# Three expert layers on one Trainium2 core: side work and low parts issued behind a row's first eviction, cosine chains shifted by a few turns

## The chip, the cores and the metric

The kernel runs on one core of one Trainium2 chip. The metric is the device time of one execution in microseconds (us), the median of several runs. The engines are TensorE (PE; its weight loads are listed as PEld), VectorE (DVE), ScalarE (ACT), GpSimd (POOL) and SyncE (SP), whose queue issues the DMAs.

## The reference, cut to what matters

```
attn = windowed attention with a linear bias, 4 batches, 8 heads, 576 positions   -> x [2304, 512]
P    = exp(x @ w_gate - max), then 8 rounds of row and column normalisation       -> P [2304, 8]
out  = sum over 8 experts e of  P[:, e:e+1] * (relu(x @ w1[e]) @ w2[e])            # w1 [512,1024], w2 [1024,512]
h    = out @ w_in                                                                   # [512, 2048]
y    = (h * cos(h)) @ w_out                                                         # [2048, 512]
```

`w_in` and `w_out` arrive as 64-bit floats.

## The kernel before, in words

After the attention stage come 120 steps in a fixed order: three token blocks of 768 tokens through the experts (32 units of 256 hidden columns each, 96 steps), then the same three blocks through the cosine layer (8 units each, 24 steps). All operands are split into a high part (rounded by a ScalarE copy) and a low part (the rest, a subtraction on VectorE or GpSimd), and every product is three matmuls: high by high, high by low, low by high.

**One step.** The first layer of a unit is a Strassen-like scheme of seven products (`product`, called with m = 5, 1, 4, 2, 3, 6, 7) of six matmuls of 384 columns each, recorded on line 759. Product 4 belongs to the unit of the step before. Between product 6 and product 7 stands `batch`: the second layer (`g2`) of an earlier unit, one step back for the experts and two for the cosine layer. It has six rows of 128 tokens (tt = 0 to 5), each of six matmuls of 512 columns (lines 863 to 865) into one PSUM bank of the pool `p_g`, which has three banks, and then one eviction (`evac`): line 854 (experts) or 844 (cosine layer) adds it to the accumulator on VectorE. Row 3 therefore needs the bank of row 0 to be read, row 4 that of row 1, and so on. All other orders are written by hand: each engine executes its instructions in the order in which the program issues them.

**After product 6** the first half of the hidden values is complete (an addition on VectorE, line 792). For the experts `relu_split` makes its high part on ScalarE (line 720) and its low part on VectorE (line 721), in front of row 0. In the cosine layer a chain (`cos_chain`) is put on the list `tail`; each call of `tick` advances every chain by one turn (up to the next `yield`): a scaled copy on ScalarE (line 731), a pair on VectorE (733, 736), the sine on ScalarE (739), a product on VectorE (742), the high part on ScalarE (746), the low part on GpSimd (748). The second half has its own chain, put there at product 4.

**Side work** stands in lists of generators, and `slot()` advances the first one of each list by one call: `pre` (splitting the weights of coming units while block 0 runs: `prep_s` on GpSimd, `prep_a` with line 132 on VectorE, `prep_b` with line 145 on GpSimd), `feed` (what the next token block needs), `bg` (first the eight normalisation rounds, whose matmul is `cs` on line 348; then `convert_f64`, which makes 32-bit weights from the 64-bit ones with seven VectorE operations, lines 218 to 238, one chunk a step) and `bg2` (splitting these weights). A slot follows each of the seven products and each of the six rows; the rows advance `pre` once more. What is left in `pre` at the end of a step is flushed. In the last step of a token block `combos` splits the next block's operands (lines 293 and 294) behind products 1, 2, 3, 6 and 7. At the end of the program two batches are left.

Of the kernel before, what the change touches and what calls it, by code (L numbers as in the profile page):

```python
# [29 lines left out]
def tile_attention_moe_cos_ffn(ctx, tc, q, k, v, w_gate, w1, w2, w_in, w_out, out):  # L30
    nc = tc.nc
    B, H, S, D = q.shape
    NT, DM = out.shape
    E, _, F = w1.shape
# [5 lines left out]
    NU1 = E * UPE  # L40
    NU2 = DFF // FU
# [8 lines left out]
    TB = 2 * HB  # L50
    NB = NT // TB
# [19 lines left out]
    with tc.manual_schedule():  # L71
# [508 lines left out]
        for hp in range(NPAIR):  # L580
            for j in range(2):
                h = 2 * hp + j
# [28 lines left out]
        for n in range(NGR + 6):  # L611
            if n < NGR:
                pi, u = groups[n]
# [76 lines left out]
        bg, bg2, pre, feed = [], [], [], []  # L690

        def step_all(lst):
            if lst and next(lst[0], StopIteration) is StopIteration:
                lst.pop(0)

        def lazy(f):
            yield from f()

        def slot():
            step_all(pre)  # L700
            step_all(feed)
            step_all(bg)
            step_all(bg2)
# [12 lines left out]
                    nc.scalar.activation(out=t[:, kc, h * HB:(h + 1) * HB], in_=ps[:, :HB], func=AF.Copy)  # L716
                    yield

        def relu_split(c, h, cols):
            nc.scalar.activation(out=h[:, 0, cols], in_=c, func=AF.Relu)  # L720
            nc.vector.scalar_tensor_tensor(  # L721
                out=h[:, 1, cols], in0=c, scalar=0.0, in1=h[:, 0, cols].bitcast(F32),
                op0=ALU.max, op1=ALU.subtract,
            )

        def cos_chain(c, new_h, tag):
            yield
            yield
            ta = u_pool.tile([P, TB], F32, tag=tag, name="ta")
            tb = u_pool.tile([P, TB], F32, tag="u0", name="tb")  # L730
            nc.scalar.activation(out=ta, in_=c, func=AF.Identity, scale=1.0 / TWO_PI, bias=quarter)
            yield
            nc.vector.tensor_scalar(
                out=tb, in0=ta, scalar1=MAGIC, scalar2=MAGIC, op0=ALU.add, op1=ALU.subtract
            )
            nc.vector.tensor_tensor(out=ta, in0=ta, in1=tb, op=ALU.subtract)
            yield
            yield
            nc.scalar.activation(out=ta, in_=ta, func=AF.Sin, scale=TWO_PI_LO)
            yield  # L740
            yield
            nc.vector.tensor_tensor(out=c, in0=c, in1=ta, op=ALU.mult)
            yield
            yield
            h = new_h()
            nc.scalar.activation(out=h[:, 0], in_=c, func=AF.Copy)  # L746
            yield
            nc.gpsimd.tensor_tensor(out=h[:, 1], in0=c, in1=h[:, 0].bitcast(F32), op=ALU.subtract)  # L748
# [16 lines left out]
        h_t = {}  # L765
# [3 lines left out]
        def product(s, m):  # L769
            kind, b, u = s  # L770
            nm = f"{kind}{b}_{u}"
            if s not in st_t:
                st_t[s] = {}
            t = st_t[s]
            lo, hi = slice(0, HB), slice(HB, TB)

            def bank(key):
                if key not in t:
                    t[key] = (p_y if key == "y" else p_xz).tile([P, 512], F32, tag=key, name=f"{key}_{nm}")
                return t[key]  # L780

            def cc(f):
                if f not in t:
                    t[f] = tp2.tile([P, TB], F32, tag=f"c{f}", name=f"c{f}_{nm}")
                return t[f]

            def keep(i, ps):
                t["s", i] = tp1.tile([P, HB], F32, tag=f"s{i}", name=f"s{i}_{nm}")
                nc.scalar.activation(out=t["s", i], in_=ps[:, :HB], func=AF.Copy)  # L789

            def add(o, ps, i):
                nc.vector.tensor_tensor(out=o, in0=ps[:, :HB], in1=t["s", i], op=ALU.add)  # L792

            def h(f):
                if (s, f) not in h_t:
                    h_t[s, f] = hp_.tile([P, 2, TB], F32R, tag=f"h{f}", name=f"h{f}_{nm}")
                return h_t[s, f]

            ps = bank({2: "x", 5: "z", 3: "z"}.get(m, "y"))
            unit_mm(ps, s, m, m in (1, 2, 5), m in (4, 2, 3))  # L800
            if m == 5:
                keep(3, ps)
            elif m == 1:
                keep(1, ps)
            elif m == 2:
                add(cc(1)[:, lo], ps, 1)
            elif m == 6:
                keep(2, ps)
                if kind == "moe":
                    add(cc(1)[:, hi], t["z"], 2)  # L810
                    relu_split(cc(1), h(0), slice(0, TB))
                else:
                    add(cc(1)[:, hi], t["z"], 2)
                    tail.append(cos_chain(cc(1), lambda: h(0), "u1"))
            elif m == 7:
                add(cc(2)[:, hi], ps, 3)
                if kind == "moe":
                    relu_split(cc(2)[:, hi], h(1), hi)
            elif m == 4:
                if kind == "moe":  # L820
                    relu_split(ps[:, :HB], h(1), lo)
                else:
                    nc.scalar.activation(out=cc(2)[:, lo], in_=ps[:, :HB], func=AF.Copy)
                    tail.append(cos_chain(cc(2), lambda: h(1), "u2"))
                del st_t[s]

        tail = []
# [40 lines left out]
        steps = []  # L868
# [18 lines left out]
        def begin_b(n):  # L887
            if n >= len(steps):
                return
            kind, b, u = steps[n]  # L890
            if b or kind == "ffn":
                load_w(u, b, "b")
            else:
                pre_next.append(prep_b(u))

        def tick():
            tail[:] = [t for t in tail if next(t, StopIteration) is not StopIteration]
# [4 lines left out]
        queue = []  # L902
        rest = []

        def batch():
            m = queue.pop(0)
            for tt in range(TPB):
                g2(steps[m], tt)
                if tt == TPB - 1:
                    begin_b(m + 2)  # L910
                slot()
                step_all(pre)
                tick()

        for n, s in enumerate(steps):
            kind, b, u = s
            pre += pre_next
            pre_next.clear()
            ph = phases.index((kind, b))
            last = n + 1 == len(steps) or steps[n + 1][:2] != (kind, b)  # L920
            nxt = phases[ph + 1] if ph + 1 < len(phases) else None
            to_end = (NU1 if kind == "moe" else NU1 + NU2) - u
            if nxt and to_end == 4:
                if nxt[0] == "ffn":
                    feed.append(x2_pieces(nxt[1]))
                    feed.append(lazy(lambda nxt=nxt: stages(nxt, x2r[nxt[1]])))
                else:
                    feed.append(stages(nxt, xr[nxt[1]]))
            nx = None
            if last and nxt:  # L930
                while feed:
                    step_all(feed)
                nx = combos(nxt, xr[nxt[1]] if nxt[0] == "moe" else x2r[nxt[1]])
            lag = 1 if kind == "moe" else 2
            for m in (5, 1, 4, 2, 3, 6, 0, 7):
                if m == 0:
                    if queue and queue[0] <= n - lag:
                        batch()
                    continue
                if m == 4:  # L940
                    if n:
                        product(steps[n - 1], 4)
                    for x in rest:
                        next(x, None)
                    rest.clear()
                    begin(n + 1)
                else:
                    product(s, m)
                tick()
                slot()  # L950
                if nx and m not in (5, 4):
                    next(nx, None)
            if nx:
                next(nx, None)
                rest.append(nx)
            queue.append(n)
            if chunk < 4 * NU2 and ((kind, b) == ("moe", 1) and u < NU1 - 5 or (kind, b) == ("moe", 2)):
                bg.append(convert_f64(chunk))
                chunk += 1
            at = n - NU1  # L960
            if 0 < at <= 5 * NU2 and at % 5 == 0:
                bg2.append(prep_ffn(NU1 + at // 5 - 1))
            while pre:
                step_all(pre)
        product(steps[-1], 4)
        while len(queue) > 1:
            batch()
        while tail:
            tick()
        batch()  # L970


# [28 lines left out]
```

## Time and profile before

| | |
|---|---|
| median of 3 runs | 2140.05 us (2138.94 to 2140.49) |
| profiled execution | 2142.25 us, span 2140.5 us |
| TensorE busy | 2073.1 us, 97% |
| VectorE, ScalarE, GpSimd busy | 1360.6, 772.9, 477.4 us |
| mean granted clock of TensorE | 0.992 |

Busy times are shares of one profiled execution, averaged over stages with different limits. An idle time that stands in square brackets behind an instruction names what ended it.

### The profile page before, as it was taken

What the parts mean: (1) busy time and instruction counts of PE and PEld (TensorE: products, weight loads), DVE (VectorE), ACT (ScalarE), POOL (GpSimd) and SP (SyncE); (2) the same over time, 40 slices, a digit from 0 to 9 for tenths busy, and PEclk for the clock granted to TensorE, in tenths of its full rate; (3) what the DMA queues carried; (4) which work ended last, traced back from release to release, by engine and by line L of the source; (5) the groups of instructions that cost most, each with busy time, mean ns of one, the idle gap of its engine ahead of it and who ended that gap; (6) DMA issues with size and microseconds to landing.
All of it is one profiled execution on the core that took longest, in us unless ns stands there. A gap on an engine that the chain in (4) does not pass through costs nothing.

```text
span 2140.5 us, 28312 instructions
## 1 busy us (share of the span) xinstructions
PE 2073.1 (97%) x10623; PEld 1818.7 (85%) x10623; DVE 1360.6 (64%) x2473; ACT 772.9 (36%) x1544; POOL 477.4 (22%) x524
## 2 busy tenths in 40 slices
PE   8989999999999999999999999999999999999998
PEld 6657889899998888888888888999989888899897
DVE  5665765666666667777776566555454465867765
ACT  6775333333343222222222222222212245555542
POOL 4342233233342002102112122110000113223221
PEclk9989999999999999999999999999999999999999
DMA  5632667777776568778787587674545445465552
GB/s 144 160 90 73 214 233 261 251 258 255 255 252 228 192 235 281 266 264 286 264 277 260 211 269 266 217 250 172 204 168 198 180 166 188 167 215 191 194 190 95
DMA packets 162105, 456.95 MB, mean 213 GB/s; under 512 B 67504, under 2 KB 106416, under 8 KB 131248
## 3 DMA queue, kind: packets, MB, share of 16 engines
q1 hardware_dynamic: 161968, 455.15, 62.3%
q8 instruction: 83, 1.36, 0.3%
q14 instruction: 54, 0.44, 0.1%
HBM read 326.65 MB, written 128.45 MB: 213 GB/s over the span
## 4 chain that ended last, share of the span: by engine, by line
PE 83%; DVE 9%; ACT 4%; issue 2%; DMA 1%; POOL 1%; POOLq 0%; ACTq 0%; SPq 0%; DVEq 0%
PE y_moe L759 18%; PE g_moe L863 10%; PE g_moe L864 9%; PE g_moe L865 9%; PE z_moe L759 9%; PE x_moe L759 4%; PE y_ffn L759 4%; PE g_ffn L865 3%; PE g_ffn L863 3%; PE g_ffn L864 3%; PE s L443 2%; PE z_ffn L759 2%; DVE h_moe L721 2%; PE x L535 2%; ACT h_moe L720 2%
## 5 line engine op out<-in xcount | busy, mean ns | idle before, releaser
L863 PE MATMUL g_moe<-wb,h_moe 128*128 128x512 f32 x1152 | 455.4, 395 | 28.4 <-DVE acc_moe L854 27.3
L865 PE MATMUL g_moe<-wb,h_moe 128*128 128x512 f32 x1152 | 452.3, 393 | 0.0
L864 PE MATMUL g_moe<-wb,h_moe 128*128 128x512 f32 x1152 | 452.3, 393 | 0.0
L854 DVE SCALAR_TENSOR_TENSOR acc_moe<-g_moe,prob,acc_moe 128x512 f32<-128x512 f32 x546 | 389.7, 744 | 97.7 <-PE g_moe L865 97.0
L720 ACT ACTIVATE h_moe<-c_moe 128x768 fp32r<-128x768 f32 x192 | 131.8, 686 | 721.5 <-DVE c_moe L792 721.5
L759 PE MATMUL y_moe<-xtT_moe,wa 128*128 128x384 f32 x1728 | 348.9, 336 | 2.6 <-DVE c_moe L792 2.2
L759 PEld LDWEIGHTS y_moe<-xtT_moe,wa 128*128 128x128 f32 x1728 | 306.0, 188 | 10.9 <-DVE c_moe L792 2.9
L863 PEld LDWEIGHTS g_moe<-wb,h_moe 128*128 128x128 f32 x1152 | 217.2, 189 | 89.4 <-DVE acc_moe L854 43.4
L865 PEld LDWEIGHTS g_moe<-wb,h_moe 128*128 128x128 f32 x1152 | 217.0, 188 | 46.6
L864 PEld LDWEIGHTS g_moe<-wb,h_moe 128*128 128x128 f32 x1152 | 217.1, 188 | 41.2
L721 DVE SCALAR_TENSOR_TENSOR h_moe<-c_moe,h_moe 128x768 fp32r<-128x768 f32 x192 | 148.5, 773 | 144.6 <-ACT h_moe L720 144.6
L789 ACT ACTIVATE s_moe<-y_moe 128x384 f32<-128x384 f32 x192 | 94.4, 492 | 276.5 <-PE y_moe L759 276.3
L120 POOL TENSOR_TENSOR s<-ra 128x256 f32<-128x256 f32 x80 | 60.6, 758 | 537.5 <-DMA ra<-w 299.9
L748 POOL TENSOR_TENSOR h_ffn<-c_ffn,h_ffn 128x768 fp32r<-128x768 f32 x48 | 89.8, 1870 | 323.9 <-ACT h_ffn L746 155.6
L721 DVE SCALAR_TENSOR_TENSOR h_moe<-y_moe,h_moe 128x384 fp32r<-128x384 f32 x96 | 53.5, 557 | 146.7 <-ACT h_moe L720 146.6
L792 DVE TENSOR_TENSOR c_moe<-z_moe,s_moe 128x384 f32<-128x384 f32 x96 | 53.4, 557 | 133.3 <-ACT s_moe L789 133.3
L863 PE MATMUL g_ffn<-wb,h_ffn 128*128 128x512 f32 x288 | 114.0, 396 | 4.6 <-DVE acc_ffn L844 2.8
L759 PE MATMUL y_moe<-xtB_moe,wa 128*128 128x384 f32 x576 | 116.4, 336 | 0.0
L759 PE MATMUL z_moe<-xtT_moe,wa 128*128 128x384 f32 x576 | 115.9, 335 | 0.0
L759 PE MATMUL x_moe<-xtB_moe,wa 128*128 128x384 f32 x576 | 115.6, 335 | 0.0
L759 PE MATMUL z_moe<-xtB_moe,wa 128*128 128x384 f32 x576 | 115.4, 334 | 0.0
L865 PE MATMUL g_ffn<-wb,h_ffn 128*128 128x512 f32 x288 | 113.7, 395 | 0.9 <-POOL h_ffn L748 0.9
(163 smaller groups left out, 3205.4 us busy)
## 6 DMA issues: line engine op xcount, KB each, us to landing
wa<-wd SPq DMA_DIRECT2D x88, 1792.0 KB, 7.5
wb<-wd SPq DMA_DIRECT2D x88, 1024.0 KB, 4.9
wd<-wa SPq DMA_DIRECT2D x32, 1792.0 KB, 6.7
wd<-wb SPq DMA_DIRECT2D x32, 1024.0 KB, 4.9
ra<-in_moe_w_dram SPq DMA_DIRECT2D x64, 256.0 KB, 7.3
rb<-in_moe_w_dram SPq DMA_DIRECT2D x64, 256.0 KB, 5.3
wd<-hla SPq DMA_DIRECT2D x48, 256.0 KB, 6.5
wd<-hlb SPq DMA_DIRECT2D x40, 256.0 KB, 8.3
```

What stands on the lines that cost most here:

```text
L120: nc.gpsimd.tensor_tensor(out=s4[:, o], in0=x, in1=y, op=op)
L443: nc.tensor.matmul(ps[:, x * 192 + c0:x * 192 + 192], qB[pi % 2][:, i, :], kT[pi][:, k0:k0 + w])
L720: nc.scalar.activation(out=h[:, 0, cols], in_=c, func=AF.Relu)
L721: nc.vector.scalar_tensor_tensor(out=h[:, 1, cols], in0=c, scalar=0.0, in1=h[:, 0, cols].bitcast(F32), op0=ALU.max, op1=ALU.subtract,)
L748: nc.gpsimd.tensor_tensor(out=h[:, 1], in0=c, in1=h[:, 0].bitcast(F32), op=ALU.subtract)
L759: nc.tensor.matmul(ps[:, :HB], wa[:, wl, WI[m], kc, :], x[:, xl, kc, :], start=start and kc == 0 and n_ == 0, stop=stop and kc == 1 and n_ ...
L789: nc.scalar.activation(out=t["s", i], in_=ps[:, :HB], func=AF.Copy)
L792: nc.vector.tensor_tensor(out=o, in0=ps[:, :HB], in1=t["s", i], op=ALU.add)
L854: nc.vector.scalar_tensor_tensor(out=a, in0=ps, scalar=pe, in1=a, op0=ALU.mult, op1=ALU.add)
L863: nc.tensor.matmul(ps, hf[f][:, 0, ts], wb[:, 0, f, :], start=f == 0, stop=False)
L864: nc.tensor.matmul(ps, hf[f][:, 0, ts], wb[:, 1, f, :], start=False, stop=False)
L865: nc.tensor.matmul(ps, hf[f][:, 1, ts], wb[:, 0, f, :], start=False, stop=f == 1)
```

## The change

Nothing is computed otherwise; the order in which instructions are issued is another. The low part behind product 6 goes on a list `later` that is emptied behind row 0's eviction (or at once where a step has no batch). The slots behind products 3 and 6 and behind row 0 are dropped, and row 0's extra call of `pre` with them. `cos_chain` gets a number of empty turns ahead as an argument (2 for the first half; 4 for the second, in the last two units 1; it was 2 for both) and one more empty turn between line 731 and the pair. At the end of the program the first of the two batches left advances the chains twice a row, behind one more turn after the last product.

```
-        def relu_split(c, h, cols):
+        later = []
+
+        def relu_split(c, h, cols, wait=False):
             nc.scalar.activation(out=h[:, 0, cols], in_=c, func=AF.Relu)
-            nc.vector.scalar_tensor_tensor(
+            low = lambda: nc.vector.scalar_tensor_tensor(
                 out=h[:, 1, cols], in0=c, scalar=0.0, in1=h[:, 0, cols].bitcast(F32),
                 op0=ALU.max, op1=ALU.subtract,
             )
-
-        def cos_chain(c, new_h, tag):
-            yield
-            yield
+            if wait:
+                later.append(low)
+            else:
+                low()
+
+        def cos_chain(c, new_h, tag, ahead):
+            for _ in range(ahead):
+                yield
             ta = u_pool.tile([P, TB], F32, tag=tag, name="ta")
             tb = u_pool.tile([P, TB], F32, tag="u0", name="tb")
             nc.scalar.activation(out=ta, in_=c, func=AF.Identity, scale=1.0 / TWO_PI, bias=quarter)
+            yield
             yield
...
-                    relu_split(cc(1), h(0), slice(0, TB))
+                    relu_split(cc(1), h(0), slice(0, TB), wait=True)
...
-                    tail.append(cos_chain(cc(1), lambda: h(0), "u1"))
+                    tail.append(cos_chain(cc(1), lambda: h(0), "u1", 2))
...
-                    tail.append(cos_chain(cc(2), lambda: h(1), "u2"))
+                    tail.append(cos_chain(cc(2), lambda: h(1), "u2", 4 if b + 1 < NB or u + 2 < NU1 + NU2 else 1))
...
-        def batch():
+        def batch(ticks=1):
             m = queue.pop(0)
             for tt in range(TPB):
                 g2(steps[m], tt)
                 if tt == TPB - 1:
                     begin_b(m + 2)
-                slot()
-                step_all(pre)
-                tick()
+                while later:
+                    later.pop(0)()
+                if tt:
+                    slot()
+                    step_all(pre)
+                for _ in range(ticks):
+                    tick()
...
                     if queue and queue[0] <= n - lag:
                         batch()
+                    while later:
+                        later.pop(0)()
                     continue
...
                 tick()
-                slot()
+                if m not in (3, 6):
+                    slot()
...
         product(steps[-1], 4)
+        tick()
+        while (steps[queue[0]], 1) not in h_t:
+            tick()
         while len(queue) > 1:
-            batch()
+            batch(2)
         while tail:
             tick()
         batch()
```

## Rows read from the trace of the kernel before

**Rows 1.** The page: busy time by engine, and one of the costliest groups.

```profile
PE 2073.1 (97%) x10623; PEld 1818.7 (85%) x10623; DVE 1360.6 (64%) x2473; ACT 772.9 (36%) x1544; POOL 477.4 (22%) x524
...
L748 POOL TENSOR_TENSOR h_ffn<-c_ffn,h_ffn 128x768 fp32r<-128x768 f32 x48 | 89.8, 1870 | 323.9 <-ACT h_ffn L746 155.6
```

**Rows 2.** Waits of TensorE: us in total, times, longest us.

```profile
PE g_moe L863 <- DVE acc_moe L854: 27.3, 37, 4.7
...
PE cs L348 <- DVE prob L341: 3.8, 4, 1.4
...
PE g_ffn L863 <- DVE acc_ffn L844: 2.8, 2, 1.4
```

**Rows 3.** Timeline of TensorE, the first product of five steps: start, us.

```profile
701.46 1.20 PE L759 MATMUL z_moe<-xtT_moe,wa 128*128 128x384 f32 x6
...
1160.08 1.20 PE L759 MATMUL z_moe<-xtT_moe,wa 128*128 128x384 f32 x6
...
1227.24 1.20 PE L759 MATMUL z_moe<-xtT_moe,wa 128*128 128x384 f32 x6
...
1325.56 1.20 PE L759 MATMUL z_moe<-xtT_moe,wa 128*128 128x384 f32 x6
...
1651.76 1.20 PE L759 MATMUL z_moe<-xtT_moe,wa 128*128 128x384 f32 x6
```

**Rows 4.** Timeline of all engines, one step with conversions.

```profile
1003.10 0.40 PE L865 MATMUL g_moe<-wb,h_moe 128*128 128x512 f32 x1
1003.32 0.84 ACT L720 ACTIVATE h_moe<-c_moe 128x768 fp32r<-128x768 f32 x1 [0.62 <-DVE c_moe L792]
...
1004.20 0.96 DVE L721 SCALAR_TENSOR_TENSOR h_moe<-c_moe,h_moe 128x768 fp32r<-128x768 f32 x1 [0.91 <-ACT h_moe L720]
...
1005.08 1.23 DVE L234 SCALAR_TENSOR_TENSOR fb<-f,fb 128x512 f32<-128x512 uint32 x1
...
1006.23 0.74 DVE L854 SCALAR_TENSOR_TENSOR acc_moe<-g_moe,prob,acc_moe 128x512 f32<-128x512 f32 x1
...
1007.02 0.50 PE L863 MATMUL g_moe<-wb,h_moe 128*128 128x512 f32 x1 [0.79 <-DVE acc_moe L854]
...
1014.12 0.42 DVE L218 TENSOR_SCALAR fa<-f 128x512 int32<-128x512 int32 x1
```

**Rows 5.** Timeline of all engines, one step of the experts' block 0.

```profile
325.55 2.40 POOL L145 TENSOR_TENSOR wb<-rb,wb 128x1024 fp32r<-128x1024 f32 x1 [2.83 <-ACT wb L143]
...
333.65 0.42 DVE L132 TENSOR_TENSOR wa<-ra,wa 128x256 fp32r<-128x256 f32 x1
...
333.98 1.22 DVE L132 TENSOR_TENSOR wa<-s,wa 128x1024 fp32r<-128x1024 f32 x1
...
334.58 0.39 PE L865 MATMUL g_moe<-wb,h_moe 128*128 128x512 f32 x1
...
337.23 1.20 PE L759 MATMUL z_moe<-xtT_moe,wa 128*128 128x384 f32 x6
```

**Rows 6.** Timeline of all engines, the last steps of the experts' blocks 0 and 1.

```profile
685.31 4.97 DVE L294 TENSOR_TENSOR xtB_moe<-xr,xtB_moe 128x768 fp32r<-128x768 f32 x2
...
694.20 0.80 PE L863 MATMUL g_moe<-wb,h_moe 128*128 128x512 f32 x1 [4.71 <-DVE acc_moe L854]
...
1220.36 0.52 PE L863 MATMUL g_moe<-wb,h_moe 128*128 128x512 f32 x1 [3.16 <-DVE acc_moe L854]
```

**Rows 7.** Timeline of all engines, the last batch.

```profile
2124.09 0.84 ACT L746 ACTIVATE h_ffn<-c_ffn 128x768 fp32r<-128x768 f32 x1 [1.28 <-DVE c_ffn L742]
2124.99 0.61 PE L863 MATMUL g_ffn<-wb,h_ffn 128*128 128x512 f32 x1 [1.84 <-ACT h_ffn L746]
...
2136.27 0.39 PE L865 MATMUL g_ffn<-wb,h_ffn 128*128 128x512 f32 x1
```

**Rows 8.** Busy time by engine (x instructions); behind POOL: granted clock, DMA share, GB/s.

```profile
2125.00:2132.00 7.00, 6.09 (x14) 4.29 (x15) 1.38 (x2) 0.00 (x0) 1.81 (x1) 0.52 0.12 44
```

**Rows 9.** The page's DMA issues: KB each, median us from issue to landing.

```profile
f<-in_moe_w_out_dram SPq DMA_DIRECT2D x16, 512.0 KB, 4.1
```

## The prediction

> **What bounds the kernel now.** I read the page first: TensorE is busy for 2073.1 of 2140.5 us [rows 1], so a change that moves work of other engines can win only the 67 us in which TensorE is not busy, and what it loses at its lower clock. The waits of TensorE come next: the largest pair is the first matmul of a `g2` row waiting for an eviction on VectorE, 27.3 us in 37 waits; the `cs` matmuls of the Sinkhorn loop wait 3.8 us, the same pair in the cosine stage 2.8 us [rows 2].
>
> Third, the starts of one product, step by step, give the price of those waits in time. From 1325.56 to 1651.76 lie 21 steps of (326.20/21 =) 15.533 us, with no wait of TensorE in them; this is the step that TensorE itself sets. The 28 steps from 701.46 to 1160.08 take 458.62 us, 23.7 more than 28 x 15.533, and the six from 1227.24 to 1325.56 take 98.32, 5.1 more than 93.2 [rows 3]. These 34 steps are those in which `convert_f64` gives VectorE extra work, and the step that precedes each run (there the conversion of `xt` is still going on). So they lose 28.8 us. From 334.58 to 337.23 lie seven `g2` matmuls and one product, 2.65 us [rows 5]; with 36 matmuls and 7 products in 15.533 us, a matmul has 0.23 and a product 1.03.
>
> Fourth, one of them in full [rows 4]. The last matmul of row 0 is issued at 1003.10 and ends at 1003.50. Its eviction runs at 1006.23, 2.7 us late, because in VectorE's queue stand ahead of it the low part of h (line 721: it waits for ScalarE's relu until 1004.16, then 0.96) and a conversion operation (line 234, 1.23). Row 3 reuses the bank of row 0 (`p_g` has three), so its first matmul starts at 1007.02 after 0.79 us of waiting.
>
> **The change in the conversion steps.** No instruction is removed; the order on VectorE's queue changes. At row 0 only the eviction is issued, then the low part, then from row 1 on the slots. By the durations of [rows 4]: eviction 1003.50 to 1004.24, low part 1004.24 to 1005.20 (relu is done at 1004.16), eviction of row 1 (its last matmul ends six matmuls after 1003.50, at 1004.88) 1005.20 to 1005.94, row 2 at 1006.24 on time. Row 3 is due 13 matmuls after 1003.10, at 1006.1, and its bank is free from 1004.24: 1.9 us to spare. A conversion operation between two evictions makes (0.74 + 1.23 =) 1.97 us against 1.37 for a row, so one row falls back by 0.6 us and the next ones, with none or a shorter one, catch up; the spare 1.9 holds it. So all 28.8 us go. Bounds: 0, if something else keeps the row waiting, and 28.8; I take 28.8, since [rows 4] leave no other instruction ahead of the eviction. The low part itself, now 0.04 us later (1004.24 for 1004.20), is read by the batch of the next step.
>
> Slots fall from 13 to 10 a step. A chunk of `convert_f64` takes ten calls (seven operations, a load, an empty call, a store), so it still ends within its step. Its load is issued at row 4 in place of row 2, 2.7 us later, behind the stores on SP's queue; it lands in 4.1 us [rows 9], from about 1009 to 1013, and the next chunk's first operation ran at 1014.12 [rows 4]: no cost. If that cover went, VectorE would wait ahead of a product's addition, which is 2 products off the next eviction.
>
> **Block 0 of the experts.** There the slots carry the splitting of the weights. `pre` needs 19 calls a step (8 of `prep_a`, 6 of `prep_b`, 5 of `prep_s`) and had 19; now it has 15, and the last four, GpSimd's, are flushed at the step's end. So the last part of `wa`, low half, moves from row 2 to row 4. In [rows 5] it starts at 333.98 and is done long before the next step's first product at 337.23. Moved: row 4's last matmul is issued at 334.58, ends at 334.97; eviction 0.74, the 256-column part (0.42), the 1024-column part (1.22) make 337.35. It is wanted by the third matmul of the product, at 337.23 + 2 x 0.17 = 337.6. So 0.2 us are left. The store of `wa` and the raw load behind it move by the same two rows on SP's queue; both are wanted a step later at the earliest. Cost 0, bounds 0 and, for 27 steps late by 0.5 us, 13 us. GpSimd's operation of 2.40 us in the same step ran at 325.55 and keeps its slot, so it does not meet these.
>
> **The first steps.** The Sinkhorn `cs` matmuls stand three calls behind the operation they need. With the calls after products 3 and 6 and row 0 gone, three calls span more TensorE work, so the 3.8 us of waits go [rows 2]; bounds 0 and 6 (other waits of these steps can go too), less what late weights take in the one or two steps with Sinkhorn work in the rows. I take 3.8.
>
> **The block changes.** In the last step of a block `combos` also stands ahead of row 0's eviction, at products 3 and 6, and stays there. TensorE waits 4.71 us at 694.20 and 3.16 at 1220.36 [rows 6]. Only the low part (0.96) or the cosine pair leaves the front, and the relu on ScalarE, ahead of the copy for `xt`, still has to be waited for. I take 1.3 for all five; bounds 0 and 5.6 (three times 0.96 and the 2.8 of [rows 2], whose two waits are of the cosine stage). The 4.71 is mostly this: two subtractions of 768 columns, two SBUF inputs each, took 4.97 us, where one of that size takes 0.96 [rows 4, 6]. The cosine chains' GpSimd part now falls beside these very operations. The Trainium skill, "SBUF — State Buffer", section "Who interferes with whom", has a rule that speaks against a gain here: VectorE instructions with two SBUF inputs and GpSimd reads share a port, one blocking the other for the whole instruction; the 4.97 us agree. By it the two cosine block changes would keep their 2.8 us, and the sum stays as I have it; without it they could give them back, and the sum would be 2.8 more.
>
> **The cosine stage.** The second chain starts two calls later and each has one empty call more, so VectorE's pair leaves the front of row 0. The low part of h1 (GpSimd, 1.87 us [rows 1]) moves from product 7 of one step to product 4 of the next, where `g2` two steps on needs it only in the sixth matmul of row 0. The cover is three products and five matmuls, (3.1 + 1.15 =) 4.2 us, against ScalarE's copy for the first half and 1.87. I cost it at nothing; where another GpSimd operation gets in, 22 steps would pay the excess.
>
> **The end.** In row 0 of the last batch TensorE waits 1.84 us, until 2124.99, for ScalarE's copy that starts at 2124.09; from there to the last matmul at 2136.27 run 32 intervals, 11.28 us where 0.23 each would give 7.4 [rows 7]. Between 2125 and 2132 the granted clock is 0.52 [rows 8]: its lower level, 1.2 GHz, after that idle time. With two calls a row the chain runs during the batch before. GpSimd's 1.87 us [rows 1] then begins about when that batch's last row ends, and its result is wanted five matmuls (1.15 us) later, 0.7 us too late; I take 1.2, because the chain's VectorE pair meets the other chain's GpSimd operation. This wait stays; the clock I take as kept, since 1.2 us is nearer to the 0.79 of [rows 4], behind which the steps of [rows 3] lose 0.85 us on average (23.7/28), than to what [rows 7] show. Gain 1.84 + 3.9 - 1.2 = 4.5; bounds 1 (the clock falls again) and 5.7.
>
> **Sum.** 28.8 + 3.8 + 1.3 + 4.5 = 38.4 us. The profiled execution took 2142.25 us, its span 2140.5; the median of three runs is 2140.05, 0.1% less. The waits do not scale with that difference, so I subtract from the median: 2101.6 us.
>
> **Rivals.**
> - *The split weights come late* in the 27 steps of block 0, by 0.2 to 0.5 us each: 5 to 13 us back, 2107 to 2115. For it: only 0.2 us of spare. Against: the durations in [rows 5] repeat step by step. 18%.
> - *The block changes and the first steps give more*: 4 to 7 us, 2095 to 2098. For it: VectorE is freer ahead of each eviction. Against: the shared work stays ahead. 12%.
> - *The conversion steps keep half of their loss*, since the same VectorE work comes in the rows instead: 14 back, 2116. Against: 1.9 us to spare. 5%.
> - *The change does nothing*: the waits go to the next eviction in line; 2140. 1.5%.
> - *Slower*: in block 0, GpSimd's operation of 2.40 us [rows 5] meets the late 1.22 us split and holds it for its whole length: 2.40 - 0.2 = 2.2 us in 27 steps, 59 us, so 2160. It decides from (38.4/27 =) 1.4 us a step. Against: the operation starts at 325.55, nine us earlier in the step, and keeps its slot. 2%.
>
> The forecast, 2098 to 2106, has the remaining 61.5%. The range from 2094 to 2110 takes in the better case and the cheaper half of the first rival, leaving about 16% out. What can be told from no change here is 0.2%, 4.3 us. Faster 0.965, same 0.015, slower 0.02.
>
> **What will show it.** Right, if the waits of `g_moe` on line 854's eviction fall from 27.3 us to about 9, those left being the block changes; if the steps of the first expert pass over converted chunks last 15.53 us; if the `cs` waits go; if the last 45 us hold no stretch at half clock. Wrong, if line 759's matmuls begin to wait for line 132 in block 0; if row 3 or 4 still waits while conversions run; or if `g_ffn` waits for GpSimd's line 748 in the middle of the cosine stage.

## The result: 1.8% faster, as forecast

The changed kernel takes 2100.89 us, the median of five runs (2097.06 to 2103.09), against 2140.05 us (2138.94 to 2140.71) of five runs of the kernel before: a ratio of 0.9816 [0.9802, 0.9831], 39.2 us. 2101.6 us was forecast, within 2094 to 2110. The span of the profiled executions falls by 41.4 us, from 2140.5 to 2099.1. Line numbers move: the first-layer matmuls stand on line 766 now, those of `g2` on 870 to 872, the evictions on 861 and 851, the low part of h on 723, the cosine pair on 740 and 743, the cosine layer's low part on 755.

The page of the changed kernel: span, and busy time by engine.

```profile
span 2099.1 us, 28328 instructions
...
PE 2059.7 (98%) x10623; PEld 1821.5 (87%) x10623; DVE 1366.0 (65%) x2473; ACT 765.0 (36%) x1544; POOL 491.4 (23%) x524
```

The matmuls are the same 10623 [rows 1]; the instructions of VectorE and GpSimd are as many as before. The waits of TensorE in the changed kernel (us in total, times, longest us):

```profile
PE g_moe L870 <- DVE acc_moe L861: 7.1, 3, 4.6
...
PE g_ffn L870 <- DVE acc_ffn L851: 2.4, 2, 1.2
PE z_ffn L766 <- DMA wa<-wd: 2.3, 1, 2.3
...
PE z_moe L766 <- DVE wa L132: 1.9, 2, 1.1
...
PE y_ffn L766 <- DVE c_ffn L799: 1.5, 2, 1.0
...
PE g_ffn L872 <- POOL h_ffn L755: 1.2, 1, 1.2
...
PE cs L348 <- DVE prob L341: 0.4, 1, 0.4
```

Beside [rows 2]: 37 waits for a `g_moe` eviction have become 3, all at block changes, and the `cs` waits are 0.4 us where they were 3.8. Three lines are new or longer: `z_moe` for line 132, `y_ffn` for line 799, `g_ffn` for line 755.

The timeline of TensorE, the first product of four steps of the changed kernel, the counterparts of the first four of [rows 3] (the last product is cut off where the view ends):

```profile
693.87 1.20 PE L766 MATMUL z_moe<-xtT_moe,wa 128*128 128x384 f32 x6
...
1128.05 1.20 PE L766 MATMUL z_moe<-xtT_moe,wa 128*128 128x384 f32 x6
...
1194.13 1.20 PE L766 MATMUL z_moe<-xtT_moe,wa 128*128 128x384 f32 x6
...
1287.17 1.03 PE L766 MATMUL z_moe<-xtT_moe,wa 128*128 128x384 f32 x5
```

The 28 steps take 434.18 us (458.62 before), the six take 93.04 (98.32): 24.4 and 5.3 us less, 29.7 of the 41.4. One of these steps in the changed kernel, timeline of all engines, the counterpart of [rows 4]:

```profile
964.87 0.40 PE L872 MATMUL g_moe<-wb,h_moe 128*128 128x512 f32 x1
...
965.31 0.75 DVE L861 SCALAR_TENSOR_TENSOR acc_moe<-g_moe,prob,acc_moe 128x512 f32<-128x512 f32 x1 [0.25 <-PE g_moe L872]
...
965.98 0.95 DVE L723 SCALAR_TENSOR_TENSOR h_moe<-c_moe,h_moe 128x768 fp32r<-128x768 f32 x1
...
966.85 0.75 DVE L861 SCALAR_TENSOR_TENSOR acc_moe<-g_moe,prob,acc_moe 128x512 f32<-128x512 f32 x1
...
967.51 0.42 DVE L230 TENSOR_SCALAR fb<-f 128x512 int32<-128x512 int32 x1
...
967.84 0.39 PE L870 MATMUL g_moe<-wb,h_moe 128*128 128x512 f32 x1
```

Row 0's last matmul ends at 965.27 and its eviction starts at 965.31, where it came 2.7 us late before. Row 3's first matmul, 967.84, has no wait. An eviction of 0.74 us that started at 967.10 would still have been in time, so by this matmul 1.83 us are to spare (forecast: 1.9); what lateness really cost is under runs 4 and 5.

By stretch of the span, from the starts of the first products of all 120 steps (step 0 is the first; the blocks change in steps 31, 63, 95, 103 and 111):

| stretch | before | after | gain | forecast |
|---|---|---|---|---|
| steps 0 to 5 (Sinkhorn) | 97.83 | 92.15 | 5.7 | 3.8 |
| steps 32 to 59 and 64 to 69 (conversions) | 556.94 | 527.22 | 29.7 | 28.8 |
| the five block changes | 93.92 | 91.79 | 2.1 | 1.3 |
| steps 96 to 99 (cosine layer begins) | 57.95 | 60.86 | -2.9 | 0 |
| from the start of step 119 | 43.9 | 39.7 | 4.2 | 4.5 |

That is 38.8 of the span's 41.4. Most of the rest lies in the other expert steps: steps 6 to 30 give 0.7 us, steps 70 to 94 give 1.5. The first and the fourth row also hold stretches at the lower clock level that fell into one of the two executions and not into the other; the points below take them apart.

### The profile page after: what moved, and what is told of

Read it like the earlier page. It is cut to its first block, busy times and chain, and to the rows that moved or that the text cites. A ratio compares the mean times of both kernels' runs of the same rounds, so it can differ in the third digit from the quotient of the medians.

```text
span 2099.1 us, 28328 instructions
## 1 busy us (share of the span) xinstructions
PE 2059.7 (98%) x10623; PEld 1821.5 (87%) x10623; DVE 1366.0 (65%) x2473; ACT 765.0 (36%) x1544; POOL 491.4 (23%) x524
## 4 chain that ended last, share of the span: by engine, by line
PE 92%; DVE 4%; ACT 1%; issue 1%; POOL 0%; DMA 0%; POOLq 0%; DVEq 0%; ACTq 0%
PE y_moe L766 18%; PE g_moe L871 12%; PE g_moe L872 12%; PE g_moe L870 12%; PE z_moe L766 9%; PE x_moe L766 5%; PE y_ffn L766 4%; PE g_ffn L872 3%; PE g_ffn L870 3%; PE g_ffn L871 3%; PE s L443 3%; PE z_ffn L766 2%; PE x L535 2%; PE x_ffn L766 1%; PE T L407 1%
## 5 line engine op out<-in xcount | busy, mean ns | idle before, releaser
L861 DVE SCALAR_TENSOR_TENSOR acc_moe<-g_moe,prob,acc_moe 128x512 f32<-128x512 f32 x546 | 407.7, 748 | 142.3 <-PE g_moe L872 138.4
L723 DVE SCALAR_TENSOR_TENSOR h_moe<-c_moe,h_moe 128x768 fp32r<-128x768 f32 x192 | 160.4, 836 | 59.9 <-ACT h_moe L722 59.9
```

The source lines that it names most:

```text
L723: low = lambda: nc.vector.scalar_tensor_tensor(out=h[:, 1, cols], in0=c, scalar=0.0, in1=h[:, 0, cols].bitcast(F32), op0=ALU.max, op1=ALU. ...
L861: nc.vector.scalar_tensor_tensor(out=a, in0=ps, scalar=pe, in1=a, op0=ALU.mult, op1=ALU.add)
```

## The experiments

Each kernel was timed in rounds against the kernel before, whose median there was 2140.4 to 2141.4 us; ratios and gains are against that. Times are medians, with the lowest and the highest run.

**1. The low part alone.** The kernel before, with only the list `later`; all slots stay.

```
+            low = lambda: nc.vector.scalar_tensor_tensor(
...
-                    relu_split(cc(1), h(0), slice(0, TB))
+                    relu_split(cc(1), h(0), slice(0, TB), wait=True)
...
+                while later:
+                    later.pop(0)()
                 slot()
```

> The kernel before with one part of the change alone: the low part behind product 6 goes behind row 0's eviction; slots, chains and the end stay. My theory (row 0's eviction needs only to come 0.8 us sooner or so, and row 3 leaves 1.9 us to spare): without the low part ahead, one conversion operation of at most 1.23 us is left in front, the bank is free by about 1005.3 where row 3 is due at 1006.1, so all of the conversion steps' loss goes, 28.8 us, and some of the block changes'; the start and the end stay as before: 2110 us. Rival (each of the two edits gives its own share): some 15 us, 2125 us.

2107.61 us (2105.08 to 2109.50), ratio 0.9845 [0.9831, 0.9860]: 33.7 us of the 39.2. Its steps in the conversion stretch last 15.51 us, but for four of 15.86 to 16.18. A conversion operation still stands ahead of the eviction there (VectorE's timeline):

```profile
965.41 0.56 DVE L798 TENSOR_TENSOR c_moe<-z_moe,s_moe 128x384 f32<-128x384 f32 x1 [0.41 <-ACT s_moe L795]
965.88 0.68 DVE L234 SCALAR_TENSOR_TENSOR fb<-f,fb 128x512 f32<-128x512 uint32 x1
966.49 0.74 DVE L860 SCALAR_TENSOR_TENSOR acc_moe<-g_moe,prob,acc_moe 128x512 f32<-128x512 f32 x1
967.15 0.95 DVE L723 SCALAR_TENSOR_TENSOR h_moe<-c_moe,h_moe 128x768 fp32r<-128x768 f32 x1
```

With the low part behind it, and with it the wait for ScalarE's relu, the eviction is no longer late enough to hold row 3.

**2. The slots alone.** The kernel before, without the slots behind products 3 and 6 and behind row 0.

```
-                slot()
-                step_all(pre)
+                if tt:
+                    slot()
+                    step_all(pre)
                 tick()
...
-                slot()
+                if m not in (3, 6):
+                    slot()
```

> The kernel before with another part alone: the slots behind products 3 and 6 and behind row 0 dropped, the low part still ahead of row 0's eviction. My theory: the low part ends at 1005.2, the eviction at 1005.9, 0.2 us ahead of row 3's due time, so the conversion steps lose nothing or almost nothing, and the Sinkhorn waits go too: 2106 to 2110 us. Rival (each gives its share): 2122 us. Another rival (no side work issued there matters, only the low part does): 2136 us.

2116.29 us (2111.41 to 2118.14), ratio 0.9879 [0.9863, 0.9896]: nearly all conversion steps go to 15.53 us too, but the whole gain, 25.1 us, is 6 to 10 short of what was expected. In its profile steps 32 and 64, the first of each conversion run, stay at 16.3 us; steps 101 and 109 grow to 16.81 each by a wait for `acc_ffn`; the last parts of the weights hold steps 3 to 5 for 2.9 us in all; and the expert steps without a wait stay at 15.533 us. The misses of the expectation are mostly these places, not the conversions.

Either edit alone takes nearly all waits out of the conversion steps. By the starts of the steps the low part alone wins 27.8 us there and the slots alone 26.3, where both together win 29.7. That answers a question that the prediction never put: its 28.8 us belong to neither edit, since each alone wins most of them, and the gains of this run, of run 1 and of run 3 add up to 61.8 us where the whole change wins 39.

**3. The cosine part alone.** The kernel before, with the shifted chains and the end.

```
-        def cos_chain(c, new_h, tag):
-            yield
-            yield
+        def cos_chain(c, new_h, tag, ahead):
+            for _ in range(ahead):
+                yield
...
         while len(queue) > 1:
-            batch()
+            batch(2)
```

> The kernel before with the cosine chains' shift and the two calls a row at the end, and nothing else. My theory: the end gives 4 to 4.5 us, the two block changes of the cosine stage under 0.5, nothing in the steps between: 2135 us, up to 3 us more where the clock falls in the first cosine steps. Rival (the chains' shift itself frees the cosine stage): 2131 us or less.

2138.35 us (2135.61 to 2143.22, ten runs), ratio 0.9991 [0.9981, 1.0]. The `g_moe` waits are those of before (26.8 us, 37 times). The end gives its four microseconds and the middle of the cosine layer takes part of them back:

```profile
PE g_moe L864 <- DVE acc_moe L855: 26.8, 37, 4.7
...
PE y_ffn L760 <- DVE c_ffn L793: 2.7, 4, 1.0
```

Step 98 lasts 16.30 us, steps 101 and 109 16.42 each, where 15.51 stood before. So the shift that was costed at nothing costs 2.6 us by itself in these three steps. It also gives: step 97 lasts 15.61 in place of 16.21, where a wait of 0.28 us for an eviction goes, and the two block changes of the cosine layer are 0.2 us shorter each. In the changed kernel steps 101 and 109 stay at 15.51; of the three only step 98 keeps the loss. The reason can be read there, in the changed kernel (timeline of all engines):

```profile
1718.84 0.55 DVE L740 TENSOR_SCALAR tb<-ta 128x768 f32<-128x768 f32 x1
1718.90 2.19 POOL L755 TENSOR_TENSOR h_ffn<-c_ffn,h_ffn 128x768 fp32r<-128x768 f32 x1 [68.16 <-ACT h_ffn L753]
1719.43 2.48 DVE L743 TENSOR_TENSOR ta<-ta,tb 128x768 f32<-128x768 f32 x1
1721.83 0.74 DVE L861 SCALAR_TENSOR_TENSOR acc_moe<-g_moe,prob,acc_moe 128x512 f32<-128x512 f32 x1
...
1723.07 0.96 DVE L743 TENSOR_TENSOR ta<-ta,tb 128x768 f32<-128x768 f32 x1
...
1725.87 1.33 PE L766 MATMUL y_ffn<-xtT_ffn,wa 128*128 128x384 f32 x6 [0.50 <-DVE c_ffn L799]
```

The second instruction of the pair (743) takes 2.48 us beside GpSimd's subtraction and 0.96 without it. What lies behind it on VectorE comes 1.5 us later, and the addition on line 799, which frees a product's bank, is late by 0.50.

**4 and 5. How late row 0's eviction may be.** The changed kernel with small VectorE operations (reductions of 144 columns, 0.33 us each, results unused) ahead of row 0's eviction in 27 conversion steps: `filler(4)` (1.3 us) in one kernel, `filler(9)` (2.99 us) in the other.

```
+                if tt == 0 and 32 <= m < 59:
+                    filler(4)
                 g2(steps[m], tt)
```

> The changed kernel with four reductions of 144 columns (some 0.33 us each, 1.3 us) put on VectorE ahead of row 0's eviction, in the 27 steps that convert one chunk each; their results are not used. My theory (row 3 leaves 1.7 to 1.9 us to spare): the time stays, 2101 us, and no wait of TensorE for these evictions appears. Rival (any work ahead of the eviction costs time, one for one): 27 x 1.1 = 30 us more, 2130 us.

> The same with nine reductions, 3.0 us. My theory: the eviction comes 2.7 us late, 1.0 us more than row 3 has to spare, so each of the 27 steps waits about 1 us and loses up to 1.3: 2128 to 2136 us. Rival (the eviction's place does not set the wait): 2101 us. Rival (one for one): 27 x 2.75 = 74 us, 2175 us.

With four: 2101.53 us (2095.82 to 2104.10), ratio 0.9809 [0.9788, 0.9830]; the steps stay at 15.51 us. With nine: 2132.15 us (2129.84 to 2134.49), ratio 0.9958 [0.9942, 0.9974]; most of the 27 steps grow by 1.15 us (33.3 in all) and the wait list looks as in [rows 2]. The timeline of VectorE and TensorE in the kernel with nine:

```profile
816.54 2.99 DVE L915 TENSOR_REDUCE fill<-logits 128x1 f32<-128x144 f32 x9
819.45 0.74 DVE L861 SCALAR_TENSOR_TENSOR acc_moe<-g_moe,prob,acc_moe 128x512 f32<-128x512 f32 x1
...
820.25 0.50 PE L870 MATMUL g_moe<-wb,h_moe 128*128 128x512 f32 x1 [0.68 <-DVE acc_moe L861]
```

and its waits of TensorE:

```profile
PE g_moe L870 <- DVE acc_moe L861: 25.8, 33, 4.6
```

Row 0 ends 7.78 us behind its step's start (965.27 less 957.49 in the changed kernel), so here at (809.05 + 7.78 =) 816.83, and the eviction is 2.62 us late, 0.79 beyond the 1.83 to spare; TensorE waits 0.68. With four the eviction starts at 815.54 in a step that begins at 806.83, 0.93 us late, and nobody waits. This turns the waits on again in the changed kernel by the lateness of that one eviction; run 4 shows that extra work on VectorE costs nothing as long as the eviction is not late enough.

How much is really to spare can be read from the steps themselves. The eviction's lateness, and what the step lasted beyond 15.507 us: 0.93 late, nothing (run 4); 1.58 late, 0.026 (kernel before, steps 72 to 90, the low part still ahead); 2.18 late, 0.54 to 0.59, and 2.73 late, 1.08 (kernel before, steps with conversions); 2.62 late, 1.15 (run 5). Lateness less loss is 1.5 to 1.65 us, not 1.83. The difference fits the weight load: in a step without a wait, the load for row 3's first matmul starts 0.22 us ahead of that matmul; in run 5 both start 0.05 us behind the eviction's end.

**6. The spare time of the split weights.** The changed kernel with three of these operations ahead of the last part of `wa` in block 0.

```
+                if i_ == 2 and 7 <= u:
+                    for _ in range(3):
...
+                        nc.vector.reduce_max(out=t, in_=logits.rearrange("p t e -> p (t e)"), axis=AX.X)
```

> The changed kernel with three reductions (1.0 us on VectorE) ahead of the last part of the split weights in block 0, in 25 steps; their results are not used. My theory (0.2 us to spare): line 766's first product waits for line 132 by about 0.75 us in each of them, 19 to 25 us in all, 2120 to 2126 us. Rival (there is more to spare than I reckoned, 1 us or more): 2101 us.

2117.74 us (2115.50 to 2118.65), ratio 0.9887 [0.9870, 0.9903]: slower than the change by 16.9 us. The 24 steps 7 to 30 last 16.21 us (+0.70; 24 times that is 16.8). One of them (all engines):

```profile
347.23 0.97 DVE L136 TENSOR_REDUCE fill<-logits 128x1 f32<-128x144 f32 x3
348.11 1.21 DVE L137 TENSOR_TENSOR wa<-s,wa 128x1024 fp32r<-128x1024 f32 x1
348.45 0.51 PE L772 MATMUL z_moe<-xtT_moe,wa 128*128 128x384 f32 x2
349.38 0.96 PE L772 MATMUL z_moe<-xtT_moe,wa 128*128 128x384 f32 x4 [0.42 <-DVE wa L137]
```

Two matmuls of the product run, the third waits for the split part, as the prediction had it. 0.97 us more in front cost 0.70, so about 0.3 were to spare, not 0.2, and the time came out below the 2120 us that were expected at least; the rival was real and missed by that much.

**7. The stall where the cosine layer begins.** The changed kernel with the last expert batch divided: rows 0 to 2 in step 96, rows 3 to 5 in step 97 (in the changed kernel step 96 has no batch and lasts 10.62 us).

```
+                    if n == len(steps) - 3 * NU2:
+                        batch(rows=range(3))
+                    elif n == len(steps) - 3 * NU2 + 1:
+                        batch(rows=range(3, TPB))
```

> The changed kernel with the batch of the last expert unit split: rows 0 to 2 in the first cosine step, rows 3 to 5 in the second, in place of all six in the second. My theory (the second step waits 2.3 us for its weights, whose load can start only at product 4 of a step without a batch, and the clock falls to its lower level after that wait in some executions, 2.9 us): the wait goes and the clock with it, 2096 to 2099 us. Rival (the weights come late for another reason, or the missing batch is paid later): 2101 us.

2093.96 us (2092.20 to 2094.60), ratio 0.9776 [0.9760, 0.9792]; 6.9 us below the change, more than expected. TensorE no longer waits for the weights of step 97 (timeline of TensorE, first products of steps 96, 97 and 99):

```profile
1692.00 1.20 PE L766 MATMUL z_ffn<-xtT_ffn,wa 128*128 128x384 f32 x6
1703.42 1.20 PE L766 MATMUL z_ffn<-xtT_ffn,wa 128*128 128x384 f32 x6
...
1730.72 1.20 PE L766 MATMUL z_ffn<-xtT_ffn,wa 128*128 128x384 f32 x6
```

From 1692.00 to 1730.72 are 38.72 us where the changed kernel takes 45.35. Of these 6.6 us, 2.8 are the clock of step 97 (last section), which the expectation had in it. The other 3.8 are three waits, 3.4 by the list, of which it had only the first: 2.27 us for the weights, 0.64 for ScalarE in step 96 and 0.50 in step 98.

**8. The block changes.** The changed kernel with the two pieces of `combos` behind products 3 and 6 moved behind rows 1 and 2.

```
+                if tt in (1, 2):
+                    for x in rowwork:
+                        next(x, None)
...
-                if nx and m not in (5, 4):
+                if nx and m not in (5, 4, 3, 6):
                     next(nx, None)
```

> The changed kernel with the two pieces of the next block's split that stand behind products 3 and 6 of a block's last step moved behind rows 1 and 2. My theory (what is left of the block changes, 6.3 and 4.1 us for the experts' and 0.9, 1.5 and 1.5 us for the others, is again the eviction of row 0 behind VectorE work, here work that GpSimd holds up): 9 to 13 us less, 2088 to 2092 us. Rival (GpSimd's hold passes on to the later evictions): 3 to 5 us less, 2096 to 2098 us. Rival (the split is needed by the next step's products, which wait instead): 2101 us or more.

2087.52 us (2085.92 to 2092.13), ratio 0.9755 [0.9742, 0.9768]: 13.4 us below the change. The waits of `g_moe` for its eviction fall from 7.1 us to 0.2; steps 31 and 63 last 16.13 and 15.50 us (21.80 and 19.56 in the changed kernel). The cosine block changes fall from 17.0 to 15.51 each, but the step behind each grows to 16.73: a new wait, of `y_ffn` for line 799, takes 2.4 of those 3.0 back. By the starts of the steps the five block changes give 13.6 us, 11.2 with that taken off; the profiled execution gains 2.4 more ahead of step 0 and 1.5 by step 97's clock, which the edit does not touch. A part of the 11.2 is the clock: no stretch at the lower level is left at steps 31 and 63, and step 63, for one, lasts 18.0 us in runs 4, 6 and 7, where the clock does not fall there, and 19.4 to 19.6 in the changed kernel and run 5, where it does.

**9. Both together.** Edits 7 and 8 in one kernel.

> The changed kernel with both moves: the split of the next block behind rows 1 and 2, and the last expert batch in two halves. If the two are independent, their gains add: 2083 to 2089 us. Rival (one takes the other's cover): 2090 us or more.

2082.67 us (2080.81 to 2084.65), ratio 0.9727 [0.9714, 0.9740]: the fastest, just under what was expected, 58 us below the kernel before and 18.2 below the change (20.3 by the sum of 7 and 8).

## Why the prediction was right, point by point

- **The conversion steps**, 28.8 forecast, 29.7 measured. The mechanism is shown: the late eviction of row 0 was the cause (run 5 brings the wait back by lateness, run 4 shows that less lateness costs nothing). The spare was mis-sized: 1.9 forecast, 1.83 by the matmul's start, 1.5 to 1.65 by what lateness cost. It was not needed, since the eviction is 0.04 us late. 0.9 of the difference is the shorter step, 34 times 0.026. What the prediction's words hide is that each of two edits nearly suffices (runs 1 and 2).
- **Block 0**, cost 0 forecast, no wait in steps 6 to 30 measured. In the changed kernel the last part of `wa` starts at 360.71, lasts 1.22 and ends as the next step's first product starts, 361.93, 0.1 us earlier than the prediction had it; the rival failed by 0.3 us (run 6).

```profile
360.38 0.41 DVE L132 TENSOR_TENSOR wa<-ra,wa 128x256 fp32r<-128x256 f32 x1
...
360.71 1.22 DVE L132 TENSOR_TENSOR wa<-s,wa 128x1024 fp32r<-128x1024 f32 x1
...
361.93 1.20 PE L766 MATMUL z_moe<-xtT_moe,wa 128*128 128x384 f32 x6
```

- **The first steps**, 3.8 forecast, 5.7 measured. Of these, 1.5 are not the change's: they are the clock in step 0. The busy times by engine of step 0, columns as in [rows 8], in the kernel before and in the changed one:

```profile
192.80:202.67 9.87, 9.09 (x43) 8.25 (x43) 3.09 (x10) 2.40 (x5) 0.00 (x0) 0.83 0.01 2
...
192.25:200.60 8.35, 7.33 (x41) 6.63 (x41) 3.09 (x10) 2.40 (x5) 0.00 (x0) 1.00 0.01 2
```

  In run 3, whose order there is that of the kernel before, step 0 lasts 8.32 us at a granted clock of 1.00. The other 4.2 us are in steps 1 to 5, close to the forecast, but as a sum of other terms: by the lists 3.4 us of `cs` waits go and another of 2.0 that was not counted (`y_moe` for an addition on VectorE, 2.2 before, 0.2 after); late weights in steps 3 and 5, as feared, take 1.9 back. That is 3.5 by the lists; the rest was not taken apart.
- **The block changes**, 1.3 forecast, 2.1 measured, 1.8 by the list of waits: 1.1 at the second of the experts' (3.16 to 2.05), 0.4 at the two of the cosine layer, 0.1 at each of the others. The first gives next to nothing (4.71 to 4.58): its step lasts 21.80 us here and 22.50 before, but 22.93 to 23.09 in runs 4, 5 and 7, which do the same there, so that the 0.7 us are within what the clock makes of this step from one execution to the next. It is still held by the shared work, as said: in the changed kernel (all engines)

```profile
677.65 1.85 POOL L267 TENSOR_TENSOR stT_moe<-xr 128x768 f32<-128x768 f32 x1 [14.83 <-DVE xtT_moe L294]
...
678.42 4.96 DVE L294 TENSOR_TENSOR xtB_moe<-xr,xtB_moe 128x768 fp32r<-128x768 f32 x2
...
679.45 3.12 POOL L145 TENSOR_TENSOR wb<-rb,wb 128x1024 fp32r<-128x1024 f32 x1
...
685.49 0.96 DVE L294 TENSOR_TENSOR xtB_moe<-xr,xtB_moe 128x768 fp32r<-128x768 f32 x1 [1.64 <-ACT xtB_moe L293]
...
686.37 0.74 DVE L861 SCALAR_TENSOR_TENSOR acc_moe<-g_moe,prob,acc_moe 128x512 f32<-128x512 f32 x1
```

  Two subtractions take 4.96 us under GpSimd's two operations, a third without GpSimd 0.96, and behind these stands the eviction. Run 8 shows the price of that order: 11 us, the clock with it. The Trainium skill, "SBUF — State Buffer", section "Who interferes with whom", has VectorE instructions with two SBUF inputs and GpSimd instructions that read SBUF shut each other out of a shared port; these durations agree, and so do the 2.48 us of step 98 (run 3). By that rule the two cosine block changes were to keep their 2.8 us of waits: they kept 2.4.
- **The cosine layer**, cost 0 forecast. Its loss of 2.9 us in steps 96 to 99 is mostly not the change's. Step 97 lasts 18.43 us against 16.20, by TensorE's clock behind the wait for `wa` (last section); where the clock stays, it lasts 15.60 (runs 5 and 6), 0.6 less than before. So the clock took 2.8, the change gave 0.6 there, and it lost 0.8 in step 98, where the chain's pair now meets GpSimd's subtraction (shown by run 3, which has the same 16.30 us). The net is near the forecast, the reasoning is not: the prediction looked at where GpSimd's low part falls, not at what the shifted pair would run beside in the middle of the layer (at the end it did), and both the loss and the gain are missing from it.
- **The end**, 4.5 forecast, 4.2 measured, and with its reasons: a wait of 1.21 us for GpSimd stays (1.2 forecast), and the clock is kept. The split of the term was not right: what the prediction takes for the clock, 3.9 us, holds a wait of 0.91 us for GpSimd that stood in the last batch of the kernel before already, so that the clock gives back some 2.8 and the wait of 1.21 is only 0.3 longer than the old one. The changed kernel's wait on TensorE's timeline:

```profile
2086.36 0.40 PE L871 MATMUL g_ffn<-wb,h_ffn 128*128 128x512 f32 x1
2087.96 0.50 PE L872 MATMUL g_ffn<-wb,h_ffn 128*128 128x512 f32 x1 [1.21 <-POOL h_ffn L755]
2088.30 0.40 PE L870 MATMUL g_ffn<-wb,h_ffn 128*128 128x512 f32 x1
```

and the busy times by engine of the 7 us around it, columns as in [rows 8]:

```profile
2085.00:2092.00 7.00, 5.79 (x26) 4.29 (x25) 3.36 (x6) 0.85 (x1) 1.81 (x1) 1.00 0.18 67
```

So the terms come out within 1 us but for the first steps (+1.9) and the start of the cosine layer (-2.9). These two are mostly the clock, 1.5 us in favour and 2.8 against, in stretches that change from one execution to the next; they partly cancel, and so part of the closeness of 2100.9 to 2101.6 is luck.

## What to carry to other kernels

Where an in-order engine empties a rotating buffer, find the first instruction that frees a buffer and put ahead of it nothing that waits for another engine; compute the slack from the next reuse (here 1.83 us by the matmul, 1.5 to 1.65 by what lateness cost) and stay below it. Before crediting a stretch with a gain, compare its granted clock in both traces. Gains of edits that remove the same lateness do not add up, so measure each alone before crediting it. Moving VectorE work with two inputs from on-chip memory costs what it newly runs beside: look for GpSimd instructions at the new place.

## What the runs showed of the hardware

**The clock behind one and the same wait.** In the changed kernel the wait for `wa` at step 97 (2.27 us; 2.38 before) is followed by products at half rate. TensorE's timeline:

```profile
1704.69 2.26 PE L766 MATMUL z_ffn<-xtT_ffn,wa 128*128 128x384 f32 x6 [2.27 <-DMA wa<-wd]
```

and the busy times by engine behind it, columns as in [rows 8]:

```profile
1706.00:1716.00 10.00, 10.00 (x43) 9.61 (x43) 3.19 (x5) 5.74 (x8) 0.00 (x0) 0.76 0.41 140
```

A product there takes 2.26 us where 1.28 stood after the same wait before, and the granted clock of the 10 us is 0.76 on average: the lower level (1.2 GHz) for part of them, the upper for the rest. Step 97 lasted 18.43 us here, 18.08 in run 4, 16.97 in run 8, 15.60 in run 5 and 15.59 in run 6, whose instructions around that step are the same and whose waits are 2.2 to 2.5 us. The same product in run 5:

```profile
1737.42 1.30 PE L766 MATMUL z_ffn<-xtT_ffn,wa 128*128 128x384 f32 x6 [2.39 <-DMA wa<-wd]
```

The clock also fell there in runs 1 and 2 (17.77 and 17.66 us), which have the cosine chains of the kernel before, and not in run 3, which has those of the change. So what decides is not the order of instructions of the change; what else does stays open. Runs 7 and 9 take the wait away, and this stretch is in neither of their traces.

**A wait costs more than its line.** Behind 2086.36 the next matmul was due at 2086.59, came at 2087.96 (1.37 late; 1.21 listed), and the one behind it 0.34 later in place of 0.23: 1.48 us in all. The first part is how the list counts, from the end of the matmul before (2086.76), which lies 0.17 us behind the time at which the next one was due. Waits of 0.50 in step 98 and of 0.42 in run 6 lengthen their steps by 0.79 and 0.70. The 34 conversion steps had one listed wait each, 19.2 us in all, and without the 0.9 us below they won 28.8: 0.28 us more for each wait. So a short wait costs some 0.3 us beyond what the list of waits says. The prediction took its largest term from the starts of the steps, which hold that, but the first steps, the block changes and what is left at the end from lists and durations.

**0.026 us a step in no list.** Expert steps last 15.507 us after and 15.533 before, with no listed wait of TensorE in either. Run 1 has the shorter step, runs 2 and 3 the longer, so it comes with the place of the low part. The timelines show where: nearly all of it lies in the matmuls of row 3, which take 1.383 us from the first to the next row's first where they take 1.360 in the changed kernel. In the longer steps row 0's eviction starts 1.58 us late, behind the low part, and ends 0.25 us ahead of row 3's first matmul; in the shorter ones it starts 0.04 late and ends 1.78 ahead. It fits the loss of the conversion steps, at its beginning, and is too short for the list, whose shortest entries are 0.2 us.
